# w_in in 256-column pieces, two first blocks on floats, half of the sign words moved, and w_out's splits pinned in place

## The chip, the cores and the metric

The kernel runs on one core of a Trainium2 chip. The metric is the device time of one execution in microseconds (us): 769.67 us is the median of three runs of the kernel before (768.7 to 769.74). The core has engines with queues of their own, which work through their instructions in order and wait for each other through semaphores: TensorE (PE in the profile; PEld is its loading of weights), VectorE (DVE), ScalarE (ACT), GpSimd (POOL) and SyncE (SP), which here issues every DMA.

## The reference

The inputs are q, k and v of 8 batches x 8 heads x 576 rows x 64 floats, p of 8 x 8 x 32 x 64 floats, and two matrices in 64-bit floats, `w_in` (512 x 2048) and `w_out` (2048 x 512).

```python
def sm_attn(qq, kk, vv):
    s = scale * np.matmul(qq, kk.transpose(0, 1, 3, 2))
    s = s - np.max(s, axis=-1, keepdims=True)
    a = np.exp(s)
    a = a / (np.sum(a, axis=-1, keepdims=True) + 1e-09)
    return np.matmul(a, vv)
p_packed = sm_attn(p, k, v)
out = sm_attn(q, p_packed, p_packed)
# x: out with heads side by side, 4608 tokens x 512
h = x @ w_in
g = h * np.tanh(softplus(h))          # Mish
return (g @ w_out).astype(np.float32)
```

Attention goes through the 32 packed rows of each head: first p against k and v, then q against the result. What follows is a two-layer network on all 4608 tokens, with Mish between the layers.

## The kernel before, in words

**Groups.** The network's hidden layer has 2048 columns, 16 blocks of 128. A group is one batch (576 tokens) and one such block; 8 x 16 = 128 groups follow each other, t = 0 to 127, batch b = t // 16 and block f = t % 16. The second attention's product with the packed values is folded into `w_in`: `packed_w` multiplies the transposed packed values `ppT` with 512 columns of `w_in` (`weave`, L584), so that a group's "up" product (`up`, L647) takes the attention weights `aT` directly. `up` runs in two halves of 288 tokens, each followed by Mish on ScalarE (L650, L652). The "down" products of the group before (`down`) stand between the halves and add into four accumulators that hold a batch's output.

**Numbers.** TensorE has a slow form for full floats and a fast one (F32R) for rounded ones. To keep precision in the fast form an operand is split into a rounded part `hi` (a copy on ScalarE) and a rest `lo` (a subtraction on VectorE), and a product becomes three: hi x hi, hi x lo, lo x hi. In batch 0, `up` uses splits of the packed weights (`part`, L595 and L596) and of `aT` (`upper` L307, `lower` L310); `down` multiplies floats there (L686), and splits (L666 to L668) in the later batches, for which `split_wo` (L106 on ScalarE, L107 on VectorE) splits w_out's 16 blocks, one call in each of the groups 14 to 29.

**64-bit weights.** The chip has no 64-bit floats, so `w_in` and `w_out` are read as pairs of 32-bit words and put together: 32 pieces of 512 numbers on each of 128 partitions (16 of `w_in`, 16 of `w_out`). `fetch` starts the DMA of a piece into one of STB = 9 staging buffers (L550, L578). `words` makes on ScalarE a scaled copy of the upper word (L557) and a rounding term from the lower one (L558, WB = 3 buffers), on GpSimd a clamp (L559) and the number's sign bit in a tile of its own (`wsign`, L562, 3 buffers). `join` shifts the bits and puts the sign in with one VectorE instruction (L566) and adds the rounding with a second (L570). A piece of `w_in` is 512 columns of one block of 128 rows, and four of them make up the columns of four groups. The list `pieces` fixes their order; in groups 0 to 13 the program joins up to piece 2t + 7 after the first half of `up` and writes the `words` up to piece 2t + 9 behind the second half.

**The opening.** Batch 0's attention stands ahead of group 0, in the order in which it is written (`first....`), with dummy products (`warm`) between. Its last steps make `aT` of the head halves g = 0 and g = 1: softmax (`peak`, `rise`, `tally`, `divide`), a transpose (`back`, L304), `upper` and `lower`.

**Later batches.** Batch b + 1's attention runs as a generator that advances between the products of batch b's groups (from group 4 on for batch 1). `load_next` issues the next tile of k, q or v of a later batch (L351, L359, with p's tile L377) when one has been used, and once in each of the groups 0 to 4.

**Order.** TensorE's order is the program's throughout. The other engines' order is the program's up to group 15 (the `by_hand` block); from group 16 on a scheduler places instructions, and may put them ahead of earlier-written ones where buffers and inputs allow, also into the stretch before.

## Time and profile before

| | |
|---|---|
| three runs | 768.7, 769.67, 769.74 us |
| the profiled execution, its own time | 767.17 us |
| its span, first to last instruction | 765.4 us |
| PE busy | 737.8 us, 96% of the span |
| DVE busy | 422.9 us, 55% |
| ACT busy | 296.3 us, 39% |
| POOL busy | 74.5 us, all of it in the first 140 us |

The profile's instructions carry the line of the kernel that issued them and names of the tiles, output first (`g<-ps_h`). Times in a timeline are the start and the duration in us from the span's start; brackets at a row's end give the idle time of the engine before the instruction and what ended it. The chain of waits is the work that ended last, followed back from the end. TensorE's busy time counts an instruction until its modelled end, and a float product of 512 columns shows as two records.

### The profile page before, as it was taken

The page shows a single profiled execution, that of the slowest core. Times are in us where ns is not written, and L with a number is a line of the kernel's source. Part 1 is how long each engine was busy: PE and PEld are TensorE (multiplying, and loading weights), DVE is VectorE, ACT ScalarE, POOL GpSimd, SP SyncE. Part 2 cuts the span into 40 slices and gives each one's busy share as a digit, 9 for nine tenths or more (in the row PEclk, how much of TensorE's full clock was granted, in tenths as well). Part 3 has the DMA queues.
Part 4 walks back from the last instruction along what each step waited for, and adds up shares of the span by engine and source line. Part 5 has one row for each costly group of instructions (what it writes and reads, how often), then busy time and mean ns, then how long its engine had stood idle before and what let it go on. Part 6 is the DMA issues. An engine that isn't in the chain of part 4 may idle for free.

```text
span 765.4 us, 12641 instructions
## 1 busy us (share of the span) xinstructions
PE 737.8 (96%) x5120; PEld 567.5 (74%) x5120; DVE 422.9 (55%) x726; ACT 296.3 (39%) x683; POOL 74.5 (10%) x70
## 2 busy tenths in 40 slices
PE   7788888999999999999999999999999999999997
PEld 6454545577788777877888778878888787888886
DVE  4867758973834647363753737463663647333232
ACT  5455736743422424243333424334332334232221
POOL 2377566000000000000000000000000000000000
PEclk9979999999999999999999999999999999999999
DMA  9999982153301433052401533032300100010002
GB/s 262 330 198 249 205 205 49 27 99 62 64 0 59 81 71 56 1 119 38 93 1 42 97 64 63 1 91 44 77 1 15 56 2 1 1 55 1 1 1 69
DMA packets 184825, 56.39 MB, mean 74 GB/s; under 512 B 173760, under 2 KB 176064, under 8 KB 184768
## 3 DMA queue, kind: packets, MB, share of 16 engines
q1 hardware_dynamic: 184768, 55.59, 31.5%
q8 instruction: 40, 0.66, 0.4%
q14 instruction: 17, 0.14, 0.1%
HBM read 46.14 MB, written 9.44 MB: 73 GB/s over the span
## 4 chain that ended last, share of the span: by engine, by line
PE 84%; POOL 6%; issue 6%; DVE 2%; ACT 1%; POOLq 0%; DVEq 0%; ACTq 0%
PE ps_h L647 24%; PE acc L666 15%; PE acc L668 14%; PE acc L667 14%; POOL wsign L562 4%; PE ps_w L584 4%; PE ps_s L406 3%; PE ps_rest L668 2%; PE ps_rest L667 2%; PE ps_rest L666 2%; PE acc L686 1%; PE ps_pp L461 1%; POOL wo L559 1%; POOL wi L559 1%; PE ps_warm L746 1%
## 5 line engine op out<-in xcount | busy, mean ns | idle before, releaser
L650 ACT ACTIVATE g<-ps_h 128x288 f32<-128x288 f32 (+1 forms) x256 | 97.3, 384 | 324.6 <-PE ps_h L647 294.3
L666 PE MATMUL acc<-wo_hi,g_hi 128*128 128x512 f32 x448 | 183.4, 409 | 0.0
L668 PE MATMUL acc<-wo_hi,g_lo 128*128 128x512 f32 x448 | 176.5, 394 | 0.0
L667 PE MATMUL acc<-wo_lo,g_hi 128*128 128x512 f32 x448 | 176.2, 393 | 0.0
L647 PE MATMUL ps_h<-aT_hi,wp_hi 128*128 128x288 f32 x512 | 166.4, 325 | 2.9 <-ACT aT_hi L307 2.9
L647 PE MATMUL ps_h<-aT_lo,wp_hi 128*128 128x288 f32 x512 | 152.0, 297 | 0.2 <-DVE aT_lo L310 0.2
L647 PE MATMUL ps_h<-aT_hi,wp_lo 128*128 128x288 f32 x512 | 151.4, 296 | 0.0
L661 DVE CAST g_hi<-g 128x512 fp32r<-128x512 f32 x112 | 47.6, 425 | 167.0 <-ACT g L650 166.8
L666 PEld LDWEIGHTS acc<-wo_hi,g_hi 128*128 128x128 f32 x448 | 83.9, 187 | 43.1 <-issue 28.7
L647 PEld LDWEIGHTS ps_h<-aT_hi,wp_hi 128*128 128x128 f32 x512 | 97.2, 190 | 21.7 <-issue 7.5
L647 PEld LDWEIGHTS ps_h<-aT_lo,wp_hi 128*128 128x128 f32 x512 | 97.2, 190 | 17.0 <-issue 7.5
L668 PEld LDWEIGHTS acc<-wo_hi,g_lo 128*128 128x128 f32 x448 | 84.0, 188 | 19.6
L647 PEld LDWEIGHTS ps_h<-aT_hi,wp_lo 128*128 128x128 f32 x512 | 97.1, 190 | 0.2 <-DVE wp_lo L596 0.2
L667 PEld LDWEIGHTS acc<-wo_lo,g_hi 128*128 128x128 f32 x448 | 84.2, 188 | 8.8
L662 DVE TENSOR_TENSOR g_lo<-g,g_hi 128x512 fp32r<-128x512 f32 x112 | 77.3, 690 | 6.4 <-DVE g_hi L661 0.5
L686 PE MATMUL acc<-wo,g 128*128 128x512 f32 x128 | 65.3, 618 | 11.5 <-DVE wo L570 8.3
L596 DVE TENSOR_TENSOR wp_lo<-ps_w,wp_hi 128x512 fp32r<-128x512 f32 x64 | 41.4, 683 | 17.6 <-ACT wp_hi L595 17.6
L595 ACT CAST wp_hi<-ps_w 128x512 fp32r<-128x512 f32 x64 | 34.5, 592 | 35.5 <-PE ps_w L584 35.5
L686 PEld LDWEIGHTS acc<-wo,g 128*128 128x128 f32 x128 | 21.8, 193 | 28.7 <-issue 15.0
L584 PE MATMUL ps_w<-wi,ppT 64*32 64x512 f32 x512 | 38.9, 600 | 0.4 <-DVE wi L570 0.3
L652 ACT ACTIVATE g_rest<-ps_h 128x64 f32<-128x64 f32 x128 | 28.1, 219 | 0.0
L562 POOL TENSOR_SCALAR wsign<-wo 128x512 f32<-128x512 f32 x16 | 27.2, 1702 | 1.3
(109 smaller groups left out, 729.6 us busy)
## 6 DMA issues: line engine op xcount, KB each, us to landing
w_st<-in_moe_w_in_dram SPq DMA_DIRECT2D x16, 512.0 KB, 6.8
w_st<-in_moe_w_out_dram SPq DMA_DIRECT2D x16, 512.0 KB, 6.2
k_n<-in_k_dram SPq DMA_DIRECT2D x56, 144.0 KB, 3.2
q_n<-in_q_dram SPq DMA_DIRECT2D x56, 144.0 KB, 3.2
v_n<-in_v_dram SPq DMA_DIRECT2D x56, 128.0 KB, 2.8
out_dram<-o SPq DMA_DIRECT2D x28, 256.0 KB, 2.0
k_t<-in_k_dram SPq DMA_DIRECT2D x4, 288.0 KB, 3.9
q_t<-in_q_dram SPq DMA_DIRECT2D x4, 288.0 KB, 9.1
```

The lines of the kernel that those rows point to most:

```text
L562: nc.gpsimd.tensor_scalar(out=self.sign, in0=self.dst, scalar1=0.0, scalar2=None, op0=ALU.mult)
L584: nc.tensor.matmul(out=ps[h * NP:(h + 1) * NP, :], lhsT=ppTb[row:row + D, g, h * NP:(h + 1) * NP], rhs=wi[c][g][row:row + D, h // 2, :], s ...
L595: nc.scalar.copy(out=hi, in_=ps)
L596: nc.vector.tensor_tensor(out=lo, in0=ps, in1=hi.bitcast(F32), op=ALU.subtract)
L647: nc.tensor.matmul(out=ps, lhsT=w[:, fs], rhs=a[:, g, cs], start=(n == 0), stop=(n == 5))
L650: nc.scalar.activation(out=self.act[:, hf * HALF:hf * HALF + m], in_=ps[:, :m], func=AF.Mish)
L661: nc.vector.tensor_copy(out=hi, in_=self.act)
L662: nc.vector.tensor_tensor(out=lo, in0=self.act, in1=hi.bitcast(F32), op=ALU.subtract)
L666: nc.tensor.matmul(out=acc, lhsT=hi[:, cs], rhs=wh, start=start, stop=False)
L667: nc.tensor.matmul(out=acc, lhsT=hi[:, cs], rhs=wl, start=False, stop=False)
L668: nc.tensor.matmul(out=acc, lhsT=lo[:, cs], rhs=wh, start=False, stop=stop)
L686: nc.tensor.matmul(out=accs[c], lhsT=grp.act[:, cs], rhs=wo[f], start=f == 0, stop=f == NF - 1)
```

## The change

Six things change together.

1. A piece of `w_in` is now 256 columns of two row blocks (`Weight(n, g)`) in place of 512 columns of one, so two pieces hold the columns of two groups. `packed_half(n)` makes the folded weights of two groups at a time, in products of 256 columns. The order of the pieces is new (two of `w_in`, then one of `w_out`, two of `w_in`, one of `w_out` for each pair of groups), and the program joins up to piece 2t + 5, one pair later than before.
2. Groups 0 and 1 multiply floats in `up` (`up_floats`, `packed_first`), with the transposed weights as they come (`floats`); the splits `upper` and `lower` of batch 0 move behind the first halves of groups 0 and 1. The last softmax step before group 0 runs in two halves, and Mish's function table is loaded ahead of group 0.
3. GpSimd makes the sign tile of every other piece only. For the others VectorE shifts (one instruction, in place) and then takes the sign from the staged upper word (a second one); the addition of the rounding is as before.
4. Staging has 8 buffers (STB), the rounding term 5 (RB), the sign tile 3 (SB).
5. `load_next` is held back: batch 1's tiles come in the groups 0, 2, 4, 5 and 6 and with the generator, and batch 2's not before group 12; what was held back is made up for afterwards.
6. The splits of w_out's blocks 2 to 15 are kept in program order on ScalarE and VectorE.

In the generator's steps, groups of odd f now advance it once, where before every fourth group did not advance it and the rest did so three times.

GpSimd's queue, pieces 2 to 5 of the list (a `wi` tile belongs to `w_in`, a `wo` tile to `w_out`). Before:

```order
L559 TENSOR_SCALAR wi_1_92<-wi_1_92 128x512
L562 TENSOR_SCALAR wsign<-wi_1_92 128x512
L559 TENSOR_SCALAR wo_232<-wo_232 128x512
L562 TENSOR_SCALAR wsign<-wo_232 128x512
L559 TENSOR_SCALAR wi_0_93<-wi_0_93 128x512
L562 TENSOR_SCALAR wsign<-wi_0_93 128x512
```

Now:

```order
L584 TENSOR_SCALAR wo_228<-wo_228 128x512
L590 TENSOR_SCALAR wsign<-wo_228 128x512
L584 TENSOR_SCALAR wi_0_91<-wi_0_91 128x512
L584 TENSOR_SCALAR wi_1_92<-wi_1_92 128x512
L590 TENSOR_SCALAR wsign<-wi_1_92 128x512
L584 TENSOR_SCALAR wo_235<-wo_235 128x512
```

Every second sign tile has gone from the queue.

VectorE's queue at the end of batch 1's attention (groups 14 and 15): `at` is the transposed weight of one head half, `aT_lo` its split, which group 16's `up` needs for both halves; `wo_lo` are w_out's splits, `r_lo` a split of the left-over tokens. Before:

```order
L304 STREAM_TRANSPOSE at<-a_1207 128x576
L107 TENSOR_TENSOR wo_lo_1478<-wo_358,wo_hi_1477 128x512
L107 TENSOR_TENSOR wo_lo_1524<-wo_413,wo_hi_1523 128x512
L107 TENSOR_TENSOR wo_lo_1577<-wo_576,wo_hi_1576 128x512
L107 TENSOR_TENSOR wo_lo<-wo_804,wo_hi 128x512
L107 TENSOR_TENSOR wo_lo_1654<-wo_579,wo_hi_1653 128x512
L107 TENSOR_TENSOR wo_lo_1710<-wo_673,wo_hi_1709 128x512
L622 TENSOR_TENSOR r_lo<-g_rest_555,r_hi 128x4x64
L107 TENSOR_TENSOR wo_lo_1772<-wo_676,wo_hi_1771 128x512
L107 TENSOR_TENSOR wo_lo_1405<-wo_232,wo_hi_1404 128x512
L310 TENSOR_TENSOR aT_lo<-at,aT_hi 128x2x288
```

Now:

```order
L326 STREAM_TRANSPOSE at<-a_1224 128x576
L332 TENSOR_TENSOR aT_lo<-at,aT_hi 128x2x288
L326 STREAM_TRANSPOSE at<-a_1224 128x576
L332 TENSOR_TENSOR aT_lo<-at,aT_hi 128x2x288
L636 TENSOR_TENSOR wp_lo<-ps_w_1447,wp_hi 128x512
L636 TENSOR_TENSOR wp_lo<-ps_w_1448,wp_hi 128x512
L114 TENSOR_TENSOR wo_lo_1472<-wo_235,wo_hi_1471 128x512
```

Of the eight splits of w_out between the second transpose and its split none stands there now: block 0's stands ahead of the softmax's last steps, the others follow later.

SyncE's queue around the end of the weights' pieces: `p_n`, `k_n`, `q_n` and `v_n` are tiles of the later batches, and the first `p_n` in both excerpts is batch 2's. Before:

```order
L578 DMA w_st<-in_moe_w_out_dram 128x1024 x2
L377 DMA p_n<-in_p_dram 32x8x32 x4
L351 DMA k_n<-in_k_dram 32x36x32 x4
L550 DMA w_st<-in_moe_w_in_dram 128x1024 x2
L377 DMA p_n<-in_p_dram 32x8x32 x4
L351 DMA k_n<-in_k_dram 32x36x32 x4
L578 DMA w_st<-in_moe_w_out_dram 128x1024 x2
L351 DMA q_n<-in_q_dram 32x36x32 x4
L578 DMA w_st<-in_moe_w_out_dram 128x1024 x4
```

Now:

```order
L573 DMA w_st<-in_moe_w_in_dram 128x2x512 x2
L618 DMA w_st<-in_moe_w_out_dram 128x1024 x2
L573 DMA w_st<-in_moe_w_in_dram 128x2x512 x2
L618 DMA w_st<-in_moe_w_out_dram 128x1024 x3
L400 DMA p_n<-in_p_dram 32x8x32 x4
L374 DMA k_n<-in_k_dram 32x36x32 x8
L374 DMA q_n<-in_q_dram 32x36x32 x8
```

Batch 2's tiles, which stood between the last eight pieces, now stand behind all of them.

The diff, cut to its core:

```diff
-STB = 9
-WB = 3
-WARM = (18, 2, 3, 12)
+STB = 8
+RB = 5
+SB = 3
+GPSIMD_SIGNS = 2
+WARM = (18, 2, 3, 12, 4)
+LOADS = {0: 1, 2: 1, 4: 1, 5: 1, 6: 1}
+LATER = 12
...
+        both = [
+            nc.scalar.copy(out=wo_hi[i], in_=wo[i]),
+            nc.vector.tensor_tensor(out=wo_lo[i], in0=wo[i], in1=wo_hi[i].bitcast(F32), op=ALU.subtract),
+        ]
+        if i >= NF - SPLIT0:
+            for x in both:
+                tc.keep_in_program_order(x)
...
+            for u in range(halves):
+                if halves > 1:
+                    self.divide(slice(g, g + 1), u)
+                nc.vector.transpose(out=self.at[:, u * n:(u + 1) * n], in_=a2f[:, u * n:(u + 1) * n])
...
-            nc.sync.dma_start(out=self.st, in_=w_in_v[:, self.m, self.c * 2 * FC:(self.c + 1) * 2 * FC])
+            nc.sync.dma_start(
+                out=self.st.rearrange("p (m x) -> p m x", m=2),
+                in_=w_in_v[:, 2 * self.g:2 * self.g + 2, self.n * FC:(self.n + 1) * FC],
+            )
...
-            nc.gpsimd.tensor_scalar(out=self.sign, in0=self.dst, scalar1=0.0, scalar2=None, op0=ALU.mult)
+            self.sign = None
+            if pieces.index(self) % GPSIMD_SIGNS == 0:
+                self.sign = stg.tile([P, FC], F32, name="wsign", bufs=SB)
+                nc.gpsimd.tensor_scalar(
+                    out=self.sign, in0=self.dst, scalar1=0.0, scalar2=SIGN_TWO, op0=ALU.mult,
+                    **({"op1": ALU.mult} if SIGN_TWO else {})
+                )
...
+            if self.sign is None:
+                nc.vector.tensor_scalar(out=bits, in0=bits, scalar1=3, scalar2=None, op0=ALU.logical_shift_left)
+                yield
+                nc.vector.scalar_tensor_tensor(
+                    out=bits, in0=self.x[:, :, 1], scalar=-0x80000000, in1=bits,
+                    op0=ALU.bitwise_and, op1=ALU.bitwise_or,
+                )
...
+        def up_floats(self, hfs, gs):
+            fs = slice(self.f * P, (self.f + 1) * P)
+            for g in gs:
+                for hf in hfs:
+                    if g == 0:
+                        self.ps[hf] = ps_h.tile([P, HALF], F32, name="ps_h", tag="ps_h")
+                    nc.tensor.matmul(
+                        out=self.ps[hf], lhsT=self.wp[:, g, fs],
+                        rhs=batches[0].floats[g][:, hf * HALF:(hf + 1) * HALF], start=(g == 0), stop=(g == 1),
+                    )
+                    if g == 1:
+                        self.mish(hf, self.ps[hf])
...
     def load_next():
-        if to_load:
+        if owed["t"] < LATER and len(to_load) <= 6 * (B - 2):
+            owed["n"] += 1
+        elif to_load:
...
-                join(2 * t + 7)
+                join(2 * t + 5 + t // 12)
```

More of the change, by code (lines that the diff above doesn't have):

```diff
@@ L791, in body @@
         first.score(0)
+        first.turn_keys(1, ("ACT", "DVE", "ACT"))
         first.spread(0)
-        first.turn_keys(1, ("ACT", "DVE", "ACT"))
         first.q_t.append(load_heads(q, 0, 1, "q_t"))
@@ L799, in body @@
         first.score(1)
+        together(first.turn_weights(0, ps_acc, ("DVE", "ACT")))
+        first.spread(1)
         words(2)
-        first.spread(1)
-        together(first.turn_weights(0, ps_acc, ("ACT", "DVE")))
         together(first.turn(0, ps_acc, ("ACT", "DVE", "ACT")))
-        words(3)
         join(1)
@@ L816, in body @@
         first.rise(slice(0, 1))
-        join(3)
-        words(4)
+        words(3)
         together(first.values(1, ps_a))
         warm(WARM[2])
+        together(first.turn_values(1, ps_a))
         first.tally(slice(0, 1))
-        together(first.turn_values(1, ps_a))
-        first.divide(slice(0, 1))
-        first.back(0)
-        first.upper(0)
         warm(WARM[2])
@@ L858, in body @@
                     kv.append(ctx.enter_context(tc.tile_pool(name="kv", bufs=2, side="left", reuse_waits="tile")))
[L859 removed]
+                owed["t"] = t
+                for _ in range(LOADS.get(t, 0)):
                     load_next()
[L861 removed]
+                if t >= LATER and owed["n"]:
+                    owed["n"] -= 1
+                    load_next()
+                grp = Group(b, f, wps[b, f // 4 if b else f // 2], g_rest)
                 grp.tiles()
```

167 lines of the change are left out of this document (103 added, 64 removed).

## The prediction

> **What bounds the kernel now.** I read the page first, then the busy time by stage, then the chain of waits of the slow stage, and last the timeline along that chain. From the page, the span:
>
> ```profile
> span 765.4 us, 12641 instructions
> ```
>
> and by stage (window: length, busy time with instruction counts of PE, PEld, DVE, ACT, POOL, then clock, DMA share, GB/s):
>
> ```profile
> 34.00:152.00 118.00, 101.22 (x559) 57.85 (x558) 86.92 (x128) 70.87 (x146) 64.17 (x55) 0.96 0.69 156
> 152.00:765.00 613.00, 608.52 (x4233) 487.74 (x4232) 314.49 (x549) 208.88 (x503) 0.00 (x0) 1.00 0.21 45
> ```
>
> From 152 us on, the seven later batches, TensorE is never free (608.5 of 613). Nothing in the change takes work from it there, so I leave those 613 us as they are. What can move lies before 152 us: the opening, and batch 0's sixteen groups. There the profile calls TensorE busy for 101 of 118 us; how much of that is work needs unit prices. The chain of waits has them where TensorE runs undisturbed (start, duration, what):
>
> ```profile
> 142.38 0.80 PE ps_h L647 x6
> 143.18 1.72 PE acc L686 x4
> ```
>
> Two halves of `up` at 0.80 and four float products of `down`, eight records at 0.43, make 5.04 us for a group. The work beside the groups, from the timeline:
>
> ```profile
> 89.56 1.09 PE L584 MATMUL ps_w<-wi,ppT 64*32 64x512 f32 x16
> 98.98 0.90 PE L461 MATMUL ps_pp<-v_n,a1T_n 128*32 128x64 f32 x40
> 108.64 0.72 PE L406 MATMUL ps_s<-xT,ppT 64*32 64x288 f32 x16
> 94.85 0.60 PE L448 MATMUL ps_a<-ident,a 128*128 128x128 f32 x4
> ```
>
> Four sets of folded weights take 4.4 us, two products with the values 1.8, four score products 2.9, the transposes some 2. With 16 x 5.04 = 80.6 that is about 92 us of TensorE work between group 0's second Mish and the end of group 16. These are the row of that Mish and the start of group 17:
>
> ```profile
> 41.56 0.35 ACT L650 ACTIVATE g<-ps_h 128x224 f32<-128x224 f32 x1
> 151.58 1.52 PE ps_h L647 x11
> ```
>
> So 110 us hold 92 us of work, and **18 us are waiting**. For what, the same chain tells between 86 and 108 us, where it hardly touches TensorE:
>
> ```profile
> 93.65 0.62 POOL wi L559
> 96.50 1.81 POOL wsign L562
> 102.66 1.82 POOL wsign L562
> 105.71 0.69 DVE wi L570
> 106.72 0.33 PE ps_ppT L472
> ```
>
> and the timeline of group 9:
>
> ```profile
> 98.59 0.68 ACT L557 ACTIVATE wo<-w_st 128x512 f32<-128x512 f32 x1
> 99.35 0.76 POOL L559 TENSOR_SCALAR wo<-wo 128x512 f32<-128x512 f32 x1 [1.04 <-ACT wo L557]
> 104.50 0.69 DVE L566 SCALAR_TENSOR_TENSOR wi<-wi,wsign 128x512 int32<-128x512 int32 x1 [1.38 <-POOL wsign L562]
> 106.72 0.33 PE L472 MATMUL ps_ppT<-ident,pp 128*128 128x128 f32 x1 [1.25 <-DVE pp L246]
> 107.89 0.36 ACT L650 ACTIVATE g<-ps_h 128x224 f32<-128x224 f32 x1 [4.83 <-PE ps_h L647]
> 108.24 0.67 ACT L557 ACTIVATE wi<-w_st 128x512 f32<-128x512 f32 x1
> ```
>
> It is a ring. ScalarE starts a pair's words only behind a group's Mish (98.59); GpSimd then needs two clamps and two sign tiles; VectorE's join stands next in its queue and waits for the last sign tile (104.50); behind the join wait `pp` and TensorE (106.72), so the next Mish is late (107.89), and the next words start at 108.24, 9.7 us after the last. GpSimd's share, from the groups of 34 to 152 us (busy us, mean ns, idle before):
>
> ```profile
> L562 POOL TENSOR_SCALAR wsign<-wo 128x512 f32<-128x512 f32 x16 | 27.2, 1702 | 1.3
> L559 POOL TENSOR_SCALAR wo<-wo 128x512 f32<-128x512 f32 x15 | 10.3, 685 | 16.6 <-ACT wo L557 14.5 <-DVE wo L566 2.1
> ```
>
> A pair costs 2 x (1.70 + 0.69) = 4.8 us, nearly a group's TensorE work, inside the ring. The DMA is busy there but not late: pieces 20 and 21 (counting from 0) are issued at 62.79, and ScalarE takes up piece 20 only at 87.11.
>
> ```profile
> 62.79 1.21 SPq L550 DMA_DIRECT2D w_st<-in_moe_w_in_dram  x2
> 87.11 0.67 ACT L557 ACTIVATE wi<-w_st 128x512 f32<-128x512 f32 x1
> ```
>
> **The opening.** Group 0's second half waits for the last split of `aT`. VectorE and ScalarE ahead of it:
>
> ```profile
> 36.21 0.77 DVE L304 STREAM_TRANSPOSE at<-a 128x576 f32<-128x576 f32 x1
> 37.01 0.67 ACT L307 CAST aT_hi<-at 128x576 fp32r<-128x576 f32 x1 [2.15 <-DVE at L304]
> 37.72 0.76 DVE L310 TENSOR_TENSOR aT_lo<-at,aT_hi 128x576 fp32r<-128x576 f32 x1 [0.74 <-ACT aT_hi L307]
> 38.83 1.28 ACT L650 ACT_TABLE_LOAD   x1
> ```
>
> Ahead of 36.21 the change takes from VectorE's queue the joins of pieces 2 and 3 (1.4 each), two `wp_lo` (0.7 each) and the first `aT_lo` (0.76): 4.9 us. Piece 1's join gains a shift, 0.4 to 0.7. So the transpose ends near 32.7 instead of 36.98. Then only one float product stands between it and Mish: 288/512 of 0.86, 0.5 us; no split, and the table is loaded. I put the second Mish at 33.5, **8 us earlier** than 41.56. What becomes late next is group 2, the first with splits. Before its `up` VectorE has joins of five pieces, two `aT_lo` and two half-size `wp_lo`: 1.4 + 2 x 3.3 + 1.5 + 0.8 = 10.3, so until 43. TensorE gets there near 40.5 (a `down` of 3.44, one `up` in floats of 1.9, folded weights 0.6, the first product of the next `down` 0.9). That gives back **2.5 us**. If the clock falls there (the stage's mean is 0.96), it is more.
>
> **The ring.** A pair now costs GpSimd 2 x 0.69 + 1.70 = 3.1 us, and with joins at 2t + 5 against words at 2t + 9 the pair that a group joins had its words two groups before, not one. Words, GpSimd and join (2.7 + 3.1 + 3.4) take 9 us, less than two groups. So VectorE should no longer wait for sign tiles, and the ring opens. **VectorE pays**: per odd piece one more instruction. Its prices:
>
> ```profile
> L566 DVE SCALAR_TENSOR_TENSOR wo<-wo,wsign 128x512 int32<-128x512 int32 x16 | 13.7, 858 | 13.2 <-POOL wsign L562 13.2
> L570 DVE CUSTOM_DVE_ANT_0 wo<-wo,wround 128x1024 uint16<-128x1024 uint16 x16 | 12.7, 806 | 0.2
> L661 DVE CAST g_hi<-g 128x512 fp32r<-128x512 f32 x112 | 47.6, 425 | 167.0 <-ACT g L650 166.8
> L107 DVE TENSOR_TENSOR wo_lo<-wo,wo_hi 128x512 fp32r<-128x512 f32 x16 | 10.0, 683 | 0.1
> ```
>
> No row shows a shift by a constant. With one input and one output of this size, as it has, the cast costs 0.43; with two inputs 0.68. I take 0.45, nearer the cast, and keep 0.86, the slowest row of the size, as the dear end. Sixteen of them are 7 us, at the dear end 14. The Trainium skill, "VectorE: DVE Perf Modes", section "The perf-mode tier table (the rule you actually need)", gives a one-source operation on 32-bit numbers in SBUF twice the rate of a two-source one; by it the shift has the cast's price and the sum stays.
>
> VectorE's 86.9 us in the stage hold 28 joins at 0.86 + 0.81 at most, 45 us, and some thirteen of w_out's splits at 0.68, 9 us, which leave the stage: 33 us of other work remain. From 43 us on it has 25 joins and 13 shifts. With undisturbed joins (1.38, the rows of 104.50 and 105.71) and shifts at 0.45 that is 34 + 6 + 33 = 73 us; with joins and shifts at the slow means 42 + 11 + 33 = 86; I take 80. TensorE has 86 us from there until group 17, at 129. Two queues nearly full and bound to each other in order do not run at the longer one's rate. The opening shows VectorE where it sets the pace:
>
> ```profile
> 20.00:40.00 20.00, 14.93 (x164) 9.97 (x163) 18.32 (x32) 10.42 (x18) 6.75 (x7) 0.93 0.95 318
> ```
>
> busy 18.3 of 20, 92%. Of the 80, some 4 come behind the last split of `aT` (folded weights, an output); 76/0.92 = 83 puts that split at 126, and the last softmax's exponential with its two table loads (1.28 each, about 3.7 in all), for which VectorE's last steps wait, at 129.5. Group 16 then takes TensorE its 5 us, so group 17 comes near 134.5. **I leave 5 us of waiting in place of the 18**; 0 if VectorE stays ahead, 12 in the first rival.
>
> **The rest.** Splitting w_out in order frees VectorE's queue ahead of group 16, but TensorE waited there for only 1.2 us, inside the 18:
>
> ```profile
> 141.26 1.12 PE L686 MATMUL acc<-wo,g 128*128 128x512 f32 x2 [1.16 <-ACT g L650]
> ```
>
> The splits then cost VectorE 0.68 a group up to group 29, where it is busy half the time (314 of 613): nothing. Batch 2's tiles wait for the weights' pieces. Tiles of k, q and p alone, by a late window of 16 us (packets, MB, share of the window):
>
> ```profile
> q1 hardware_dynamic: 8768, 1.10, 43.5%
> ```
>
> take 6.96 us per 1.10 MB, so 8 us for a batch's p and k (1.3 MB). The last piece is fetched behind group 9's join. At 86/14.6 = 5.9 us a group from 43 us on, that is near 88; it lands near 91, p 1 us later, k by 100. VectorE meets batch 2's p in group 10 (90 to 93 us), k in groups 12 and 13 (102 and 108). Covered, for p barely: a wait of 1 or 2 us is within the 5. Floats and fillers cost TensorE 0.8 us. Pieces of `w_in` now come in rows of 2,048 bytes, not 4,096. The nearest rows, of 1,536 bytes, make up most of the first 20 us:
>
> ```profile
> 0.00:20.00 20.00, 16.04 (x181) 14.08 (x181) 8.34 (x27) 9.65 (x22) 6.28 (x12) 1.00 0.95 262
> ```
>
> 262/0.95 = 276 GB/s against 397 for pieces alone (4.04 MB in 10.2 us, last row of the rivals), so a piece costs between 1.3 and 1.9 us, sixteen up to 9 us more. With 4,096 and 2,048 bytes so near I take them as equal; at the dear end p would land some 8 us late, and what VectorE does not make up of it is the upper half of my range.
>
> **Sum.** -8 (opening) + 2.5 (group 2) - 13 (18 less 5) + 1 = **-17.5 us** on the profiled span of 765.4, so 748. The profiled execution itself took 767.17, the median of the runs is 769.67; the same difference from the median gives **752.2 us**.
>
> **Rivals.** *VectorE becomes the bound* (18%): 82/0.92 = 89 us of it end at 132, with 3.7 for the exponential and 5 for group 16 at 141, so 12 us of waiting are left instead of 5: -10.5, 759.2. For it speaks that joins beside GpSimd cost 858 ns against 683 for a subtraction of that size; against, that GpSimd's work falls by a third. The Trainium skill, "SBUF — State Buffer", section "Who interferes with whom", says that GpSimd and a VectorE operation in a two-port mode, or with two SBUF inputs, lock each other out for a whole instruction. By that rule the new shifts wait too, which is this rival; the trace agrees as far as L566 goes. *Everything hides* (8%): no waiting left, -22.5, 747. *The ring closes again* (5%), through the 5 rounding buffers, whose writer on ScalarE stands ahead of Mish and waits for the join of the same group: time as before, 769.7. Before, with three buffers, that wait was rare (us in total, times, longest):
>
> ```profile
> ACT wround L558 <- DVE wo L570: 2.1, 1, 2.1
> ```
>
> *Slower* (6%): short rows make `w_in`'s pieces dear on the DMA, the last piece lands late, and VectorE's transposes of batch 2's p and k, which stand between joins, stop its queue. It decides from the point where p lands some 17 us behind group 10's join, that is the last piece near 110 instead of 91. Sixteen pieces cost 1.3 us each as they are (23 to 33 us, a stretch of pieces alone); doubled, they come 21 us later: 774.
>
> ```profile
> q1 hardware_dynamic: 1108, 4.04, 101.7%
> ```
>
> **Numbers.** The forecast has 63%; its own range is 748 to 757. Runs of this kernel tell apart about 0.2%, 1.5 us. Faster: 63 + 18 + 8 = 89%; within: 5%; slower: 6%. The range of 745 to 762 takes in the VectorE rival and the hidden case.
>
> **What would show it.** Second Mish of group 0 at 33 to 35 us; VectorE's waits for w_out's `wsign` down from 13.2 us to under 3; group 17 near 134 instead of 151.6, and from there on 613 us as before; a shift at 0.43 in its row; VectorE over 85% busy from 43 us to there. I am wrong if TensorE still waits for joins in groups 6 to 12, if VectorE stands at batch 2's p, or if the splits slow the groups after 16.

## The result

The changed kernel takes 762.34 us (median of five runs, 758.85 to 763.39); the kernel before, run beside it, 768.7 (five runs, 767.46 to 769.74). The ratio is 0.9907, with a 95% interval of 0.9877 to 0.9936: 0.9% faster, 6.4 us. The prediction was 752.2 us, 17.5 less than before; its sign was right, its size was not, and the time lies just above its range. Here and below, single runs of 1,017 to 4,037 us, far off all others of their kernel, are left out.

The profiled execution took 758.85 us. It is the fastest of the five. Its span, from the page, and two windows of it (length, busy time with counts of PE, PEld, DVE, ACT, POOL, then clock, DMA share, GB/s):

```profile
span 757.0 us, 12758 instructions
```

```profile
35.00:143.00 108.00, 99.87 (x614) 56.09 (x615) 88.81 (x138) 63.38 (x140) 45.73 (x41) 0.98 0.75 185
143.00:757.00 614.00, 607.77 (x4223) 486.27 (x4222) 320.48 (x560) 213.81 (x513) 0.00 (x0) 1.00 0.21 44
```

As a ruler for the stages serves one short instruction in each group: the Mish of its left-over tokens, right behind that of its second half. In the timeline of the kernel before, for groups 0, 5, 12 and 17:

```profile
41.80 0.22 ACT L652 ACTIVATE g_rest<-ps_h 128x64 f32<-128x64 f32 x1
...
77.83 0.22 ACT L652 ACTIVATE g_rest<-ps_h 128x64 f32<-128x64 f32 x1
...
130.15 0.22 ACT L652 ACTIVATE g_rest<-ps_h 128x64 f32<-128x64 f32 x1
...
153.52 0.22 ACT L652 ACTIVATE g_rest<-ps_h 128x64 f32<-128x64 f32 x1
```

and of the changed one, for the same groups:

```profile
35.08 0.23 ACT L727 ACTIVATE g_rest<-ps_h 128x64 f32<-128x64 f32 x1
...
72.28 0.22 ACT L727 ACTIVATE g_rest<-ps_h 128x64 f32<-128x64 f32 x1
...
116.72 0.22 ACT L727 ACTIVATE g_rest<-ps_h 128x64 f32<-128x64 f32 x1
...
143.03 0.22 ACT L727 ACTIVATE g_rest<-ps_h 128x64 f32<-128x64 f32 x1
```

So the change is 6.7 us ahead at group 0, only 5.6 at group 5, 13.4 at group 12, 10.5 at group 17, and 8.4 at the end of the span. Between groups 5 and 12 it won 7.9 us; before and behind them it lost.

Where it lost before group 5 the timeline shows. Two instructions of TensorE that waited long (the brackets), and VectorE around them:

```profile
45.37 1.10 PE L761 MATMUL acc<-wo,g 128*128 128x512 f32 x2 [2.98 <-DVE wo L610]
67.67 1.53 PE L624 MATMUL ps_w<-wi,ppT 64*32 64x256 f32 x16 [2.63 <-DVE a L449]
```

```profile
41.51 1.09 DVE L605 SCALAR_TENSOR_TENSOR wo<-wo,wsign 128x512 int32<-128x512 int32 x1
42.52 0.68 DVE L600 SCALAR_TENSOR_TENSOR wo<-w_st,wo 128x512 int32<-128x512 int32 x1
43.12 2.10 DVE L610 CUSTOM_DVE_ANT_0 wo<-wo,wround 128x1024 uint16<-128x1024 uint16 x2
...
62.01 0.38 DVE L598 TENSOR_SCALAR wo<-wo 128x512 int32<-128x512 int32 x1
...
64.34 1.70 DVE L610 CUSTOM_DVE_ANT_0 wo<-wo,wround 128x1024 uint16<-128x1024 uint16 x2
65.96 0.81 DVE L445 TENSOR_REDUCE mx<-ps_s 128x1 f32<-128x288 f32 x2
67.00 0.94 DVE L449 TENSOR_SCALAR a<-ps_s,top 128x288 f32<-128x288 f32 x2
```

The first is `down` of group 1, which waits for block 1 of w_out; its join runs interleaved with that of block 2, which nothing needs before group 3. The second is the folding of the next weights: its two PSUM buffers hold batch 1's scores, and the subtraction that frees them (67.00) stands behind a whole pair of joins (62.01 to 66). Behind this stop TensorE runs at a lower clock:

```profile
68.00:73.00 5.00, 5.00 (x27) 2.49 (x26) 3.34 (x7) 1.62 (x6) 0.00 (x0) 0.70 1.03 221
```

From 73 to 120 us there is hardly a gap:

```profile
73.00:120.00 47.00, 46.63 (x352) 26.39 (x352) 38.49 (x62) 29.39 (x64) 23.59 (x22) 1.00 0.80 201
```

### The profile page after: what moved, and what is told of

Read it like the earlier page. It is cut to its first block, busy times and chain, and to the rows that moved or that the text cites. A ratio compares the mean times of both kernels' runs of the same rounds, so it can differ in the third digit from the quotient of the medians.

```text
span 757.0 us, 12758 instructions
## 1 busy us (share of the span) xinstructions
PE 737.0 (97%) x5184; PEld 566.2 (75%) x5184; DVE 431.4 (57%) x750; ACT 296.1 (39%) x691; POOL 53.7 (7%) x54
## 4 chain that ended last, share of the span: by engine, by line
PE 85%; DVE 4%; DMA 4%; ACT 4%; issue 1%; SPq 1%; POOL 0%; DVEq 0%
PE ps_h L706 24%; PE acc L741 15%; PE acc L743 13%; PE acc L742 13%; PE ps_w L624 4%; PE acc L761 4%; PE ps_s L429 2%; DMA q_t<-in_q_dram 2%; PE ps_rest L743 2%; PE ps_rest L742 2%; PE ps_rest L741 2%; PE ps_pp L484 2%; DMA out_dram<-o 1%; PE ps_a L471 1%; DMA q_n<-in_q_dram 1%
## 5 line engine op out<-in xcount | busy, mean ns | idle before, releaser
L706 PE MATMUL ps_h<-aT_hi,wp_hi 128*128 128x288 f32 x504 | 161.9, 321 | 0.3 <-ACT g L725 0.3
L706 PE MATMUL ps_h<-aT_hi,wp_lo 128*128 128x288 f32 x504 | 148.3, 294 | 0.6 <-DVE wp_lo L657 0.6
L706 PE MATMUL ps_h<-aT_lo,wp_hi 128*128 128x288 f32 x504 | 148.4, 294 | 0.0
L706 PEld LDWEIGHTS ps_h<-aT_hi,wp_hi 128*128 128x128 f32 x504 | 94.8, 188 | 17.1 <-issue 4.3
L706 PEld LDWEIGHTS ps_h<-aT_lo,wp_hi 128*128 128x128 f32 x504 | 94.8, 188 | 15.9 <-issue 6.7
L706 PEld LDWEIGHTS ps_h<-aT_hi,wp_lo 128*128 128x128 f32 x504 | 94.5, 188 | 1.0 <-DVE wp_lo L657 1.0
L636 DVE TENSOR_TENSOR wp_lo<-ps_w,wp_hi 128x512 fp32r<-128x512 f32 x56 | 36.1, 684 | 17.6 <-ACT wp_hi L635 17.6
L624 PE MATMUL ps_w<-wi,ppT 64*32 64x512 f32 (+1 forms) x576 | 39.1, 559 | 4.7 <-DVE a L449 3.8
L635 ACT CAST wp_hi<-ps_w 128x512 fp32r<-128x512 f32 x56 | 30.1, 590 | 32.8 <-PE ps_w L624 32.8
L761 PEld LDWEIGHTS acc<-wo,g 128*128 128x128 f32 x128 | 21.4, 190 | 22.9 <-issue 13.2
L743 PE MATMUL ps_rest<-wo_hi,r_lo 128*128 128x512 f32 x64 | 25.1, 392 | 0.0
```

The source lines that it names most:

```text
L624: nc.tensor.matmul(out=ps[h * NP:(h + 1) * NP, :], lhsT=ppTb[row:row + D, g, h * NP:(h + 1) * NP], rhs=w[row:row + D], start=True, stop=Tr ...
L635: nc.scalar.copy(out=hi, in_=ps)
L636: nc.vector.tensor_tensor(out=lo, in0=ps, in1=hi.bitcast(F32), op=ALU.subtract)
L706: nc.tensor.matmul(out=ps, lhsT=w[:, fs], rhs=a[:, g, cs], start=(n == 0), stop=(n == 5))
L743: nc.tensor.matmul(out=acc, lhsT=lo[:, cs], rhs=wh, start=False, stop=stop)
L761: nc.tensor.matmul(out=accs[c], lhsT=grp.act[:, cs], rhs=wo[f], start=f == 0, stop=f == NF - 1)
```

## The experiments

All medians in one place; ratios are to runs of the kernel before taken beside them.

| | us | ratio, 95% interval |
|---|---|---|
| changed kernel, first five runs | 762.3 | 0.9877 to 0.9936 |
| the same again, `a_again` | 761.0 | 0.988 to 0.993 |
| `x_warm` | 763.3 | 0.9897 to 0.9941 |
| `x_open` | 761.5 | 0.9881 to 0.9941 |
| `x_no_sign` | 757.6 | 0.9824 to 0.9877 |
| `x_flush_first` | 762.1 | 0.9889 to 0.9934 |
| `x_flush5` | 758.6 | 0.9839 to 0.9877 |
| `x_defer` | 756.6 | 0.9826 to 0.9874 |
| `x_both` | 752.2 | 0.9762 to 0.98 |
| `x_both_out3` | 752.2 | 0.9767 to 0.982 |
| `x_no_pin` | 767.4 | 0.9962 to 0.9996 |
| `x_gp_signs` | 763.7 | 0.9909 to 0.9959 |
| `x_gp_pin` | 756.8 | 0.9818 to 0.9865 |
| `b_signs` | 775.2 | 1.0061 to 1.0109 |
| `b_signs_pin` | 765.1 | 0.994 to 0.9977 |
| `x_both_pin` | 752.6 | 0.9765 to 0.981 |
| `x_both_gp_pin` | 755.9 | 0.9794 to 0.9848 |
| `x_near` | 775.5 | 1.0075 to 1.014 |
| `x_near_gp` | 777.2 | 1.0088 to 1.0125 |

The eleven runs of the changed kernel have their median at 762.0. Where a sentence below gives a lead at a group, it is read from the ruler, against the changed kernel's first profile.

**Why one kernel takes 758 to 764 us** (`a_again`, no edit).

> The changed kernel once more, unaltered, since its five runs lie 4.5 us apart (758.85 to 763.39) and only the fastest has been seen in a profile. Theory: the first 165 us repeat within 0.5 us, and the spread is made of waits of about 1 us in the later batches, where the folded weights on TensorE wait for the score subtraction on VectorE and that stands behind the copy of an output tile whose buffer waits for its DMA (in the profiled execution once, at 324 us: 0.94 us). Expected: 759 to 763 us, the first group of batch 1 at 143 us, and as many such waits as the span is us above 756. Rival: the spread is in the opening's DMA; then group 0's second Mish moves by 1 us or more and the time after group 17 repeats (614 us).

Its profiled execution took 764.21 us, span 762.4. The rival was right: of the 5.4 us 4.8 arise before group 2 (3.3 of them by group 0), the lag is 5.1 at group 17, and the rest repeats. Windows of both profiles, the first one's ahead:

```profile
20.00:25.00 5.00, 4.24 (x79) 3.59 (x76) 3.74 (x8) 3.66 (x8) 0.34 (x1) 1.00 1.02 352
25.00:30.00 5.00, 4.17 (x58) 3.26 (x57) 4.83 (x10) 1.56 (x4) 1.76 (x2) 1.00 1.04 394
```

```profile
20.00:25.00 5.00, 4.58 (x62) 3.36 (x66) 3.70 (x6) 2.47 (x7) 0.00 (x0) 0.68 1.04 333
25.00:30.00 5.00, 5.00 (x78) 4.09 (x71) 2.25 (x7) 1.58 (x3) 2.10 (x2) 0.64 1.04 396
```

and two rows of the second profile's timeline:

```profile
18.11 0.66 ACT L582 ACTIVATE wi<-w_st 128x512 f32<-128x512 f32 x1 [2.91 <-DMA w_st<-in_moe_w_in_dram]
20.12 0.72 PE L163 MATMUL ps_s<-qT,ppT 64*32 64x288 f32 x16 [1.69 <-ACT qT L146]
...
48.73 1.70 PE L761 MATMUL acc<-wo,g 128*128 128x512 f32 x2 [2.99 <-DVE wo L610]
```

ScalarE waits for the second piece of w_in, qT's copies stand behind, TensorE stands idle, and two microseconds later its clock is halved. The stop in group 2 is the same in both profiles (2.98 and 2.99 us); in the first the clock stayed up behind it (1.00 from 45 to 50 us), here it fell (0.64 from 48 to 52). Two edits were to test this opening.

```diff
         join(2)
-        warm(WARM[2])
+        warm(WARM[2] + 5)          # x_warm
```

> The changed kernel with five more dummy products on TensorE ahead of the first scores of the second attention (about 1.4 us of them). The two executions of the changed kernel that were profiled differ by 5.4 us, all of it before 50 us: 3.3 by group 0's second Mish, after which one shows the granted clock at 0.50 from 22 to 28 us, behind a TensorE that stood idle for 1.69 us at 18.4. Theory: that idle time lowers the clock, and the clock makes the difference; with dummies there every execution runs like the fast one: group 0's second Mish at 35 to 36 us, the median of 762.0 (eleven runs) falls to 758.5 to 760, and the runs lie within 2.5 us of each other. Rival: the late w_in piece itself costs the 3 us (ScalarE's copies of qT stand behind its words), the clock only goes with it: median and spread as they were, 761 to 763.

```diff
         first.spread(1)
-        words(2)
         together(first.turn(0, ps_acc, ("ACT", "DVE", "ACT")))
+        words(2)                   # x_open
...
+        warm(5)
         together(first.turn(1, ps_acc, ("ACT", "ACT", "ACT")))
```

> The changed kernel with the words of the second w_in piece behind the copies of qT on ScalarE, and five dummy products ahead of the second turn of q. Theory: the change issues that piece's DMA behind q's and v's, so that ScalarE waits for it (1.0 us in one profile, 2.9 in the other) with qT's copies behind, and TensorE behind those; with the copies ahead TensorE no longer waits there, and the dummies keep the clock up while q's second half lands (21.7 to 22.5 us): second Mish at 34 to 35.5 us in every execution, the median falls from 762.0 to 758 to 759.5. Rival: the words of the piece are then late for its join, which stands on VectorE ahead of the softmax of the second head half, and the time stays at 761 to 763.

Neither made the kernel faster beyond the noise. Both profiles have the full clock up to 45 us and group 0 at 36.2 (`x_warm`) and 35.4 us (`x_open`); the theory that every slow execution has its loss there falls. In both, the clock fell behind the stop in group 2 (0.81 and 0.71 from 45 to 50 us) and cost 1.7 and 1.6 us. `x_warm` lost 2.7 more at group 19, where VectorE waited to copy an output tile and the folded weights behind it:

```profile
DVE o L750 <- DMA out_dram<-o: 2.0, 1, 2.0
PE ps_w L624 <- DVE a L449: 1.9, 1, 1.9
```

**The two stops.** First the work that VectorE does there: `x_no_sign` leaves the sign out.

```diff
                 yield
-                nc.vector.scalar_tensor_tensor(
-                    out=bits, in0=self.x[:, :, 1], scalar=-0x80000000, in1=bits,
-                    op0=ALU.bitwise_and, op1=ALU.bitwise_or,
-                )
```

> The changed kernel without the instruction that puts the sign into the odd pieces on VectorE; half the weights lose their sign, so the output is another. VectorE loses 16 instructions of 0.75 to 1.1 us, about five of them ahead of 68 us. Theory: up to 68 us VectorE is the bound as a whole, so the lead at group 5 grows by 4 to 5 us, and the time falls by 4 to 6 (756 to 758 at the median). Rival: VectorE holds TensorE only at two places by its order, where one or two of these instructions stand ahead: 1 to 2 us. Second rival: the bound there is the DMA of the pieces and of batch 1's tiles (busy 93 to 103% of those windows): nothing.

The median fell by 4.5; in the profile the lead was 2.3 us at group 2, 5.8 at group 5 and 4.5 at the end. That is what both the first theory and a mere shortening of the two stops give. The next edits keep all the work and change its order.

```diff
+            if chunk:
+                flush()            # x_flush_first; x_flush5: if t == 5
             if t <= 13:
```

> In the odd groups of batch 0 the pending steps of batch 1's attention are placed on VectorE ahead of the group's joins instead of behind them. Theory: the stop of TensorE at 64.4 to 67.7 us comes from the order alone: the two buffers that the folded weights need hold batch 1's scores, and the subtraction that frees them stands behind a pair of joins (4 us). Then 2.8 us of waiting and some 2 us of halved clock behind it go: the step from group 4 to 5 falls from 11.2 to 6.5 to 8 us, and the time by 3 to 5 us (757 to 759 at the median). Rival: VectorE is the bound as a whole there (13.4 of 15 us busy from 53 to 68); the joins then come 2 us later, a later group takes the wait, and the time falls by 0 to 1 us.

The stop at 64 us went (from group 4 to 5 the lead grew by 4.5 us), and between groups 7 and 8 a new one took it all back (4.9 us):

```profile
79.42 1.35 DVE L461 TENSOR_REDUCE rs<-a 128x2 f32<-128x1152 f32 x1 [4.40 <-ACT a L457]
...
84.47 1.10 PE L761 MATMUL acc<-wo,g 128*128 128x512 f32 x2 [3.65 <-DVE wo L610]
```

The edit had also put the sum of batch 1's first softmax ahead of the joins, where it waits for ScalarE's exponential and its table. So the same edit in group 5 alone:

> As the kernel with the pending steps ahead of the joins, but in group 5 alone. There the stop at 64 us went (lead 3.7 us at group 5) and came back as 3.65 us in group 7, where the sum of the first softmax, placed ahead of the joins, waited 4.4 us for ScalarE's exponential and its table load. Theory: each of these stops is set by what stands ahead of a join or a score step in VectorE's order, not by VectorE's whole work; with the sum behind the joins again the 3.7 us stay: median 758 to 759 (762.0 less 3 to 4). Rival: VectorE or the DMA of the pieces is the bound by then, and the gain is used up by group 9 whatever the order: 761 to 762.5.

4.5 us won between groups 4 and 5, nothing given back, 758.6. VectorE had the same instructions; only their order differed. The other stop:

```diff
-                join(2 * t + 5 + t // 12)
+                join(6 if t == 1 else 2 * t + 5 + t // 12)   # x_defer
...
                 wps[0, f // 2 + 1] = packed_half(f // 2 + 1)
+                if t == 1:
+                    join(7)
```

> The changed kernel with the join of w_out's block 2 moved in group 1 from beside block 1's join to behind the split of aT and the split of the next folded weights; down needs block 1 at 41.8 us, where TensorE waits 3.15 us, and block 2 only one group later. VectorE then reaches the end of that wp_lo some 2.5 us earlier. Theory: the step from group 1 to 2 falls from 9.4 us by 2 to 2.5, and the time by 1.5 to 2.5 (median 759.5 to 760.5) unless the next stop (64 us, five joins later) takes it, VectorE having the same work up to there. Rival, VectorE bound as a whole up to 68 us: the lead at group 2 is there and is gone at group 5: 761.5 to 762.5.

The median fell by 5.4 us, over twice what the theory gave. In the profile the stop shrank from 2.98 to 1.08 us and the lead at group 2 was 2.0, as expected:

```profile
43.35 1.10 PE L761 MATMUL acc<-wo,g 128*128 128x512 f32 x2 [1.08 <-DVE wo L610]
```

Of the other 3.4 us the clock accounts for 1.3 to 2.8. Of eight profiles in which this stop lasts 2.98 or 2.99 us (the changed kernel's two, `x_flush_first`, `x_flush5`, `x_warm`, `x_open`, `x_no_pin`, `x_near`) the clock fell in seven, and these lost 1.3 to 2.8 us more from group 1 to 2 than the first profile, which alone escaped. It escaped by chance. In every profile the clock changes only at points 3.41 us apart, and where these points lie in the span differs from execution to execution. In the seven, 1.78 to 2.99 us of the stop lie between two such points, and at the second the clock halves. In the first profile a point (43.73 us) falls into the stop and leaves 1.34 us of it on one side and 1.64 on the other. The two periods of that profile around its stop, and then the end of the stop and the period behind it in `x_warm`:

```profile
40.32:43.73 3.41, 2.07 (x12) 0.68 (x4) 3.41 (x5) 3.00 (x8) 3.33 (x4) 1.00 1.02 388
43.73:47.14 3.41, 1.77 (x7) 1.12 (x8) 3.41 (x6) 0.67 (x1) 2.76 (x2) 1.00 0.82 126
```

```profile
44.72:48.13 3.41, 1.63 (x6) 0.98 (x7) 3.41 (x6) 0.67 (x1) 2.90 (x3) 1.00 1.01 141
48.13:51.55 3.42, 3.42 (x9) 1.87 (x7) 3.42 (x7) 0.41 (x1) 0.00 (x0) 0.50 0.94 338
```

In the seven with a stop of 1.08 to 1.41 us there (`x_defer`, `x_both`, `x_both_out3`, `x_both_pin`, `x_gp_signs`, `x_gp_pin`, `x_near_gp`) it stayed at 1.00. The Trainium skill, "TensorE: Matmul & The Clock Gate", section "HAM oscillation — how this bites in real kernels", gives the rule "no PE-idle gaps >~3.4µs"; here a stop of 2.99 us was enough in seven of eight profiles.

Both edits together, and with a third output buffer (`OB = 3`) against waits like that at group 19:

> The changed kernel with both single edits that gained: block 2's join moved in group 1, and the pending score steps ahead of the joins in group 5. Theory (two stops, each set by one place in VectorE's order, each lowering the clock behind it): the gains add. Against the fast profile of the changed kernel the leads were 2.0 us at group 2 and 4.5 us from group 4 to 5, so its profile should lead by 5.5 to 6.5 us at group 5 and keep it to the end, and the median be 752.5 to 755. Rival (VectorE's whole work up to 68 us is a second bound just behind): the joins for groups 3 to 6 are then late, and the pair gains no more than the better one alone, 756 to 757.

> The same with three output buffers in place of two. In four of nine profiles of the changed kernel and its variants TensorE's folded weights in group 3 of a later batch waited 0.9 to 2.1 us more than their usual 0.3, for a score subtraction that stood on VectorE behind the copy of an output tile whose buffer waited for its DMA (up to 2.0 us). Theory: with a third buffer these waits go, 0.5 to 1.5 us below x_both and a narrower spread. Rival: the copies wait for TensorE's last products of the batch and the DMA only rarely decides: the same as x_both within 0.5 us.

The gains add: 752.2, in four runs from 752.0 to 752.4, 2.2% below the kernel before and 1.3% below the changed one. The profile leads by 6.8 us at group 5 and 6.7 at the end. From 35 to 73 us, the changed kernel first:

```profile
35.00:73.00 38.00, 31.49 (x161) 16.72 (x162) 33.58 (x51) 20.48 (x49) 22.14 (x19) 0.96 0.96 241
```

```profile
35.00:73.00 38.00, 36.04 (x201) 19.68 (x200) 37.12 (x60) 24.11 (x55) 26.37 (x23) 1.00 0.96 250
```

TensorE is busy 36.0 instead of 31.5 us; VectorE, which also looked nearly full before, does more too. The third output buffer changed nothing in the median: it took VectorE's and ScalarE's waits for an output's DMA from 15.4 us to 1.3 in the span behind 143 us, so these waits decided little, as the rival has it. Its runs spread more, not less (751.0 to 755.9).

**The splits in program order.**

```diff
-        if i >= NF - SPLIT0:
+        if False:                  # x_no_pin
```

> The changed kernel without the sixth part: w_out's splits are left to the scheduler. Twelve of them then stand on VectorE between the sums of batch 1's last softmax and the split of its transposed weights, 12 x 0.69 = 8.3 us. Theory: TensorE now reaches group 16 with VectorE's last steps as the only thing late, so the start of batch 1 moves by 6 to 8 us and the time with it (768 to 770 at the median), with nothing won back later. Rival, the sentence of the prediction: TensorE waited there for only 1.2 us before, so at most 1 us (762 to 763.5).

5.4 us slower at the median. Its profile has a slow opening like `a_again`'s, so it is compared with that one: 6.7 us are lost at group 14, and 5.7 remain at the end. On VectorE, ScalarE and TensorE:

```profile
132.79 2.49 DVE L114 TENSOR_TENSOR wo_lo<-wo,wo_hi 128x512 fp32r<-128x512 f32 x4
...
142.74 0.72 ACT L329 CAST aT_hi<-at 128x576 fp32r<-128x576 f32 x1 [1.94 <-DVE at L326]
143.34 0.35 ACT L725 ACTIVATE g<-ps_h 128x224 f32<-128x224 f32 x1
...
143.75 2.07 PE L761 MATMUL acc<-wo,g 128*128 128x512 f32 x2 [6.08 <-ACT g L725]
```

The way differs from the expectation's: TensorE stops not at group 16's `aT_lo` but two groups earlier, at group 14's Mish, which stands on ScalarE behind the casts of w_out's splits and behind `aT_hi`, which waits for VectorE and the splits there.

**The signs and the ring.** The third part undone (`GPSIMD_SIGNS = 1`), and made alone in the kernel before (`words` and `join` as in the change, every second piece):

> The changed kernel without its third part: GpSimd makes the sign tile of every piece, VectorE loses 16 shifts of 0.41 us. Theory (the ring of the prediction is still there with one pair more of lookahead): GpSimd, busy 8.75 of the 9 us from 34 to 43, has 1.8 us more for each of the pieces 3 and 5, so the join of w_out's block 1 comes 3 to 4 us later and TensorE's stop at 41.8 us grows by that much; later groups need 4.8 us of GpSimd for each pair beside 5 to 6 of TensorE, and some of the waits of the kernel before return: 765 to 768 at the median. Rival: it was the lookahead that opened the ring; VectorE, relieved of 6.6 us, gains: 759 to 761.

> The kernel before with the third part of the change alone: every other sign word on VectorE. Theory (the ring through GpSimd made the 17 us of waiting before group 17): VectorE's waits for sign tiles (21.5 us from 42 to 152) fall below 5, and the time by 5 to 8 us (761 to 764). Rival: with the joins still one pair behind the words, each join waits for the words and clamps of its own group, and the sign tile was only the last link: VectorE waits for the clamp instead and the time falls by 0 to 2 us (767 to 769).

Both were disturbed by one and the same thing. In the kernel before, with the signs:

```profile
81.52 0.45 DVE L390 STREAM_TRANSPOSE pT<-p_n 128x256 f32<-128x256 f32 x1 [7.52 <-DMA p_n<-in_p_dram]
```

```profile
82.57 0.67 ACT L557 ACTIVATE wround<-w_st 128x512 int32<-128x512 uint32 x1 [6.11 <-DVE wi L581]
```

```profile
83.28 2.04 PE L697 MATMUL acc<-wo,g 128*128 128x512 f32 x2 [8.12 <-ACT wround L557]
```

Batch 2's p, which the scheduler puts between two steps of a join, stops VectorE, then ScalarE, whose rounding buffer waits for the join, then TensorE. In `x_gp_signs` the same transpose waited 4.90 us between groups 8 and 9. The prediction's slower rival had this chain, through short rows; here the order made it. So both once more, with the transpose kept in program order:

```diff
+            if self.b == 2:
+                tc.keep_in_program_order(x)   # x: the transpose of p
```

> The changed kernel with all sign tiles on GpSimd again, and the transpose of batch 2's p kept in program order. Without the pin that transpose had been placed ahead of a join in group 8 and waited 4.9 us for p's DMA; up to group 8 the kernel was as early as the changed one (0.1 us ahead), after it 5 us behind. Theory (one more pair of lookahead opened the ring; whose engine makes the sign does not matter): 758.5 to 761.5, no later than the changed kernel at 762.0, and no waiting of VectorE for sign tiles over 3 us after group 2. Rival (the signs on GpSimd close the ring in the later groups): 763 to 766.

> The kernel before with every other sign on VectorE, and the transpose of batch 2's p kept in program order. Without the pin the time was 775.2, with one stop of TensorE of 8.3 us at 74.6 us: that transpose stood between two steps of a join and waited 7.5 us for p's DMA. Theory: the stop and the halved clock behind it were the whole loss, and the signs alone gain 0 to 2.5 us, since each join still stands one pair behind its words: 766 to 769. Rival (the prediction's ring through GpSimd): with the stop gone the signs show their worth: 761 to 764.

With all signs on GpSimd the changed kernel is not slower but faster, 756.8 against 762.0, by more than expected: its stop in group 2 is 1.41 us long, and the clock stays up behind it. On VectorE the two pairs of joins ahead of that place take 3.2 and 4.1 us there, against 5.1 and 4.4 in the changed kernel. The pin alone was not run on the changed kernel. VectorE's only wait for a sign tile from 73 to 143 us:

```profile
DVE wo L607 <- POOL wsign L592: 0.4, 1, 0.4
```

In the kernel before, signs and pin together gain 3.4 us (765.1), between the ranges of theory and rival; the pin alone was not run there either. VectorE still waits 13.9 us for sign tiles, against 21.5 without the edit. And on the better version:

> The version with both gaining edits (752.2), and the transpose of batch 2's p kept in program order. There it waited 2.4 us for its DMA, but TensorE did not stop in that group. Theory: VectorE has reserve by then, so nothing changes: 751.5 to 753. Rival: the wait pushes VectorE's later steps up to the end of batch 1's attention, which TensorE meets at 128.6 us (0.86 us): 750 to 751.5.

> The same with all sign tiles on GpSimd, so that VectorE loses 16 shifts of 0.41 us, 6.6 us in all, some 3 us of them before 73 us, where it was busy 37.1 of 38 us. Theory (VectorE is what is left as the bound up to there): 749.5 to 751.5. Rival (GpSimd's sign tiles, 1.8 us each beside VectorE, make the joins of groups 0 to 2 late, as the first stop of the version with all signs there came 1.3 us later): 753 to 756.

The pin changes nothing there (752.6); with GpSimd's signs it is slower, 755.9 in four runs from 752.4 to 756.6. The rival's times came; its place was not seen, as there is no profile of an execution of that length.

Last, the lookahead, taken away from group 6 on (with all signs on GpSimd in `x_near_gp`; the pin in both):

```diff
-                join(2 * t + 5 + t // 12)
+                join(2 * t + 5 + t // 12 + (2 if t >= 6 else 0))
```

> The changed kernel with the one more pair of lookahead taken back from group 6 on (joins up to piece 2t + 7 there, one pair behind the words, as before the change), batch 2's p pinned. The signs stay as changed. Theory (the lookahead opened the ring): from group 7 to 12 the kernel takes more than the 31.2 us of the changed one, towards the 37.3 of the one before: 34 to 37, VectorE waits for GpSimd's tiles in each group again, and the time is 764 to 768. Rival (moving the signs opened it): 31 to 32 us for these groups, apart from one extra pair of joins of 4 us in group 6, and 760 to 763.

> The same with all sign tiles on GpSimd: both halves of the ring as before the change, from group 6 on. Theory (lookahead alone counts): 35 to 38 us from group 7 to 12 and 764 to 769, within 2 us of the version above. Rival (with the lookahead away, GpSimd's 4.8 us a pair decide): 37 to 40 us, and 3 us or more slower than the version above.

From group 7 to 12 the two take 43.4 and 45.4 us, more than any theory gave; the changed kernel and `x_gp_pin` take 31.2, the kernel before 37.4. The ring stands in rows of the first: VectorE's join waits for GpSimd, and TensorE for the split behind that join.

```profile
100.33 0.69 DVE L607 SCALAR_TENSOR_TENSOR wi<-wi,wsign 128x512 int32<-128x512 int32 x1 [2.29 <-POOL wsign L592]
...
103.22 0.90 PE L486 MATMUL ps_pp<-v_n,a1T_n 128*32 128x64 f32 x40 [2.15 <-DVE wp_lo L659]
```

In these groups of the changed kernel the lookahead is worth 12 to 14 us with either way of making signs, the signs 2 us or nothing. In neither run does ScalarE wait for a piece's DMA from 60 to 140 us, so the ring goes through the engines. That it is slower there than the kernel before (37.4) is not explained: the extra pair of joins in group 6 may be part of it, but that share was not measured apart, and the order of the pieces, the buffers and the held-back loads were not undone one by one.

## Why the prediction was wrong

**The ring, right in place, half right in cause.** "18 us of waiting" was read nearly right. From the ruler of group 0 to that of group 16, before and after:

```profile
41.80:151.88 110.08, 96.39 (x544) 54.41 (x543) 80.59 (x118) 65.41 (x137) 59.96 (x52) 0.98 0.68 155
```

```profile
35.08:140.82 105.74, 97.61 (x601) 54.04 (x601) 87.24 (x135) 61.93 (x136) 45.65 (x41) 0.98 0.75 185
```

TensorE is idle for 13.7 us before; with half of the 5.2 us that it was busy at the halved clock that is 16.3 us lost. VectorE no longer waits for w_out's sign tiles from 43 us on, as predicted, and from group 5 to 12 TensorE's waits are gone. But the step credited GpSimd's lighter pair ("A pair now costs GpSimd 2 x 0.69 + 1.70 = 3.1 us") together with the lookahead; of the two, the runs give it to the lookahead.

**"I leave 5 us of waiting in place of the 18": the step that failed.** With the 2.5 of group 2 the sum left 7.5 us; by the same addition the profile has 9.8, and `a_again` 11.6. They are 0.9 us ahead of 39.8, 3.0 ahead of 45.4, 2.6 ahead of 67.7 with 1.7 of low clock behind, and 1.6 in single waits in groups 7 to 15. The stop in group 5 was not foreseen: the price of a busy VectorE was spread over the stage as a rate (92%), whereas it lay in what stood ahead of one subtraction. The "group 2" term had the right group, and its list of VectorE's work was right, but its prices were those of an undisturbed VectorE. What it put at 10.3 us took 14.0, beside a GpSimd that was busy for 13.2 of them:

```profile
32.98:46.97 13.99, 8.95 (x41) 4.31 (x41) 13.32 (x18) 10.55 (x23) 13.20 (x11) 1.00 0.91 243
```

The two pairs of joins took 5.1 and 4.4 us instead of 3.3, the splits of `aT` 1.16 instead of 0.76; and TensorE met this at the first product of `down`, which the working had let pass. TensorE also did 2.1 us more work (95.9 for 93.8), not 0.8. So the stage gained 4.3 us (110.1 to 105.7) instead of 9.5: 1.7 us because less was lost before than read, 2.3 because more is lost now, 1.3 by work. In the profiled execution 5.2 of the 9.1 us that are missing lie here, 1.3 in the opening and 2.7 behind group 16; at the median 2.0 more are missing, as the changed kernel's median lies further above its profiled execution (3.5 us) than the other's (1.5).

**The clock.** "If the clock falls there … it is more" stood in the prediction without a price. It fell there in seven of the eight profiles with that stop, at 1.3 to 2.8 us each. Of the changed kernel itself only two executions were profiled. Of its eleven runs the two fastest have a mean granted clock of 0.998, as in the profile in which it did not fall there, and the other nine 0.991 to 0.996; that points the same way, but does not show the place.

**The opening** ("8 us earlier"): 6.7 in the first profile, 3.4 in the second. The mechanism is that predicted; that the change fetches the second piece later, with qT's copies behind it on ScalarE, was not weighed.

**"From there on 613 us as before"**: 616.2 from group 16 on against 613.5; 14 pinned splits now stand in groups 16 to 29, where without the pin it is 614.8. "Nothing" was some 1.5 us: groups 16 to 20 take 20.3 and 20.4 us in the two profiles of the changed kernel, 18.8 without the pin and 18.5 before. Another 0.9 us is lost behind group 20, where the first profile has a single wait of that length at 324 us. The same pin saves some 7 us ahead of group 16, where the prediction saw only 1.2: that wait was short because TensorE came late.

**Prices.** VectorE from 43 to 134 us as a window, and two of its groups there and over the span (busy us, mean ns, idle before):

```profile
43.00:134.00 91.00, 85.06 (x545) 47.51 (x546) 76.01 (x121) 50.05 (x109) 37.89 (x34) 0.98 0.77 184
```

```profile
L598 DVE TENSOR_SCALAR wo<-wo 128x512 int32<-128x512 int32 x7 | 2.9, 409 | 1.5 <-POOL wo L584 1.5
```

```profile
L736 DVE CAST g_hi<-g 128x512 fp32r<-128x512 f32 x112 | 47.6, 425 | 167.3 <-ACT g L725 167.1
```

The shift took 0.41 us (0.45 assumed), and ahead of 43 us, beside GpSimd, 0.82 and 0.83. The Trainium skill, "VectorE: DVE Perf Modes", section "The perf-mode tier table (the rule you actually need)", had it at the cast's price, and the trace agrees (cast 0.425). VectorE's 76 us were below the 80 assumed (of which 2 came from a slip: 28 joins at 1.67 us are 46.8 and not 45, which leaves 31 of other work). So *VectorE becomes the bound* is not the reason either: `x_both` has the same VectorE work and is 10 us faster. *The ring closes again* did not come in the change; its rounding buffers stopped ScalarE in `b_signs`. Short rows of w_in cost nothing that a run shows; batch 2's p made VectorE wait 1.1 us.

That `x_both` lands on the predicted 752.2 us does not confirm the sum: it gets there with two edits that the prediction did not contain.

## What to carry to other kernels

A busy share says how full an in-order engine is, not whom it makes wait: for each instruction that another engine waits for, add up what stands ahead of it in the queue, and move what nobody needs yet behind it. Look at single stops of TensorE before rates, since a stop that leaves TensorE idle for half of a 3.41 us period is paid twice, by the wait and by the clock behind it. When two parts of a change are meant to open the same ring, predict each with the other taken away.

## What the runs showed of the hardware

The granted clock takes two values in the nineteen profiles, 1.00 and 0.50, and changes only at points 3.41 us apart. It fell 39 times. In 38 of them TensorE had been idle for 1.71 to 3.41 us since the point before, in one (`x_no_pin`) for 1.53. Of the periods behind which it stayed at 1.00, three had 1.81 to 1.85 us of idle time and all others at most 1.64. (TensorE's ends are modelled, and so are these idle times.) So about half a period of idle time, summed over its gaps, halves the clock, and not the length of one gap: in the opening it fell after gaps of 1.69 (`a_again`) and 1.78 us (`x_gp_signs`) and after four of 0.61 to 0.76 in a row (`x_no_pin`), but not after single ones of 1.36 or 1.37 in four profiles, nor after the 2.98 us of the first profile, which two periods shared.

One instruction on VectorE has two prices: in the changed kernel 1.09 us at 41.51, while GpSimd makes a sign tile, and 0.68 at 47.23, with GpSimd idle. Beside GpSimd it is not always the dear one: the instruction at 42.52 took 0.68 with GpSimd busy throughout. Nor is VectorE shut out for the whole of GpSimd's instruction, as the prediction's first rival took it: the one at 41.51 ends at 42.60, the sign tile at 42.93 (GpSimd's spans are rough).

```profile
47.23 0.68 DVE L605 SCALAR_TENSOR_TENSOR wi<-wi,wsign 128x512 int32<-128x512 int32 x1
```

```profile
41.39 1.54 POOL L590 TENSOR_SCALAR wsign<-wi 128x512 f32<-128x512 f32 x1
```

From group 20 to the end the nineteen profiles, of all kernels, take 594.8 to 596.3 us: what tells them apart happens in the first 180 us, and for the two executions of the changed kernel 4.8 of 5.4 us in the first 55.
